# One fused attention and token-mixing kernel: the band of batch 0 added to its scores by matmuls, the local result turned mostly by whole-array matmuls, and another order of all steps

## The chip, the cores and the metric

The kernel runs on one core of one Trainium2 chip, as one program. The metric is device time in microseconds (us) of that core. Engines are named as in the profile: PE (TensorE matmul), PEld (its weight loads), DVE (VectorE), ACT (ScalarE), POOL (GpSimd), and SP, whose queue issues nearly all DMA transfers.

## The reference, cut to what matters

Inputs are q, k and v of 8 batches, 8 heads, 576 positions and head size 64, all float32, and four weights.

```python
def sm_attn(qq, kk, vv):                      # softmax(qq kk^T / 8) vv
    ...
q_d, k_d, v_d = means over groups of 4 positions
out_up    = np.repeat(sm_attn(q_d, k_d, v_d), 4, axis=2)
mask      = np.abs(pos[:, None] - pos[None, :]) < 4
scores    = np.where(mask, scale * np.matmul(q, k.transpose(0, 1, 3, 2)), -1e9)
out_local = np.matmul(softmax(scores), v)
x = (out_up + out_local).transpose(0, 2, 1, 3).reshape(B, S, H * D)   # 8 x 576 x 512

theta  = x @ w_theta                                                  # 512 x 512
zr, zi = x * np.cos(theta), x * np.sin(theta)
y = np.einsum('ts,bsd->btd', w_tok_r, zr) + np.einsum('ts,bsd->btd', w_tok_i, zi)
u = x + y
return u + np.maximum(u @ w_ch, 0.0)
```

So each position attends to at most seven neighbours (the band of half-width 3), and a coarse attention over 144 means is added to that. The result x goes through a phase mixing over the positions, and then over the channels.

## The kernel before, in words

Everything is computed in bfloat16 with float32 sums in PSUM. PSUM is one tile `PS` of 8 banks, and every step is told which banks it uses. The work of a batch is cut into small steps, each a function with a name of two letters:

- Loading: `lk`, `lq` (288 KB each, four per batch) and `lv`, `lw` (two halves of one chunk of v, 128 KB each) are issued on SP into 16 staging slots `st`. `ck`, `cq`, `cv` cast them to bfloat16 on DVE, ACT or POOL. For batch 0, v comes by `l1`, `c1`, `t1`, `e1`, `x1` instead.
- `tp` (line 302) transposes q and k by nine 128x128 matmuls; `ev` (line 315) copies the result from PSUM to `qT`, `kT`. Batch 7 does this by DMA (`dk`).
- Coarse attention: `qd`, `kd` (means), `pv`, `vd` (means of v), `sd` (scores, line 426), `ed` (exp, line 437), `nd` (times v, lines 447 and 452), `xn` (divide), `xd`, `xc` (turned, into `xdT`).
- Local attention: the 576 positions are cut into 10 blocks of 58 own positions, each seen through a window of 64; two blocks make a chunk, and the five chunks make three units of 2, 2 and 1 chunks. `ps` (line 482) makes the scores of a unit by matmuls of 64x64 on a quarter of the PE array. `ex` (line 490) takes the exponential of it all on ACT; `mk` (line 503 on POOL, line 505 on DVE) multiplies by `band`, a 0/1 tile. `po` (line 515) multiplies by v and, through a column of ones, makes the sums; `nm` (lines 523, 524) divides into `tmp`. `xt` (line 537) turns `tmp` so that channels lie on the partitions, again by 64x64 quarter-array matmuls; `xa` (line 545) adds the coarse result and writes `xT`.
- Mixing: `th` (line 556) and `tt` make theta, `cs` and `ct` its cosine and sine on ACT, `xm` turns x back, `zz` and `zt` (line 577) multiply, `mx` (line 636) mixes over positions with nine 128x128 by 288 matmuls, `ua` (line 641) adds x. `up`/`uc` or a DMA transpose `du` turn u, `ch` (line 666) multiplies by w_ch, `rl` (line 674) adds, `st` stores. `ht`, `rt`, `ss`, `sr` do the same for the last 64 positions of two batches together.
- The weights w_tok are loaded (`la`, `lb`, `lc`) and transposed (`wp`, `wc`) in the first part of the program. `wm` (line 764) are matmuls on a zero tile whose result nobody reads.

The order is written out by hand in the string `ORDER`: each word is a step's kind, then the PSUM banks, the engine or the staging slot. The n-th word of a kind is the n-th step of that kind (batch by batch). Each engine executes its instructions strictly in the order of the words, and waits where an operand isn't there yet or a buffer isn't free. Before the words, `constants` prepares `ident`, `band` and the rest. `te` and `ts` load ACT's tables.

## Time and profile before

| | |
|---|---|
| time, median of 3 runs | 230.32 us (229.73 to 231.82) |
| span of the profiled execution | 232.2 us |
| PE, PEld busy | 217.7 us (94%), 152.6 us (66%) |
| DVE busy | 187.7 us (81%) |
| ACT busy | 156.2 us (67%) |
| POOL busy | 145.0 us (62%) |
| HBM read, written | 33.98 MB, 9.44 MB |
| instructions | 9404 |

The profiled execution is known by its span, from the first to the last instruction of the trace; the page gives no other time for it. The span is 1.9 us (0.8%) longer than the median of the runs, and 0.4 us longer than the longest of them. Busy times count a matmul from its start to the modelled end of its pipeline, so neighbouring steps overlap: what a step costs PE is read from start to start. All places in the program are given in us from the start of the span.

### The profile page before, as it was taken

What the parts mean: (1) busy time and instruction counts of PE and PEld (TensorE: products, weight loads), DVE (VectorE), ACT (ScalarE), POOL (GpSimd) and SP (SyncE); (2) the same over time, 40 slices, a digit from 0 to 9 for tenths busy, and PEclk for the clock granted to TensorE, in tenths of its full rate; (3) what the DMA queues carried; (4) which work ended last, traced back from release to release, by engine and by line L of the source; (5) the groups of instructions that cost most, each with busy time, mean ns of one, the idle gap of its engine ahead of it and who ended that gap; (6) DMA issues with size and microseconds to landing.
All of it is one profiled execution on the core that took longest, in us unless ns stands there. A gap on an engine that the chain in (4) does not pass through costs nothing.

```text
span 232.2 us, 9404 instructions
## 1 busy us (share of the span) xinstructions
PE 217.7 (94%) x3943; PEld 152.6 (66%) x3970; DVE 187.7 (81%) x367; ACT 156.2 (67%) x243; POOL 145.0 (62%) x192
## 2 busy tenths in 40 slices
PE   7997899999999999899999989989998999999992
PEld 3655678877877666776775675756655775668741
DVE  5699888999988799789968887698986978558473
ACT  4589799689988898898877978778788232430000
POOL 7689977879985999879963489598952001100000
PEclk9999799999999999999999999999999999999999
DMA  6999968997999689968999996892284358656587
GB/s 217 395 390 390 291 114 238 361 300 118 265 391 179 165 245 285 243 142 214 205 165 347 307 213 115 206 153 92 67 149 109 71 127 193 138 159 137 142 227 245
DMA packets 76795, 49.41 MB, mean 213 GB/s; under 512 B 61136, under 2 KB 61392, under 8 KB 76752
## 3 DMA queue, kind: packets, MB, share of 16 engines
q1 hardware_dynamic: 76096, 47.76, 81.9%
q10 hardware_dynamic: 656, 1.05, 1.3%
q8 instruction: 31, 0.51, 0.9%
q14 instruction: 12, 0.10, 0.1%
HBM read 33.98 MB, written 9.44 MB: 187 GB/s over the span
## 4 chain that ended last, share of the span: by engine, by line
PE 60%; DMA 10%; POOL 10%; issue 6%; ACT 5%; DVE 4%; SPq 4%; DVEq 0%; POOLq 0%; ACTq 0%
PE PS L636 21%; PE PS L666 9%; PE PS L556 8%; DMA st<-in_q_dram 6%; PE PS L302 4%; POOL two L329 3%; PE PS L515 2%; SPq L347 2%; DMA st<-in_k_dram 2%; PE PS L537 2%; DMA ur<-uT 2%; POOL q_tm L295 2%; PE PS L482 2%; PE PS L447 1%; PE PS L595 1%
## 5 line engine op out<-in xcount | busy, mean ns | idle before, releaser
L636 PE MATMUL PS<-WT,z 128*128 128x288 bf16 x576 | 78.0, 287 | 0.0
L636 PEld LDWEIGHTS <-z 128*128 128x128 bf16 x576 | 53.9, 98 | 15.9 <-issue 1.3
L641 DVE TENSOR_TENSOR uT<-PS,xT 128x288 bf16<-128x288 f32 x64 | 28.6, 452 | 12.7 <-PE PS L636 10.9
L561 ACT ACTIVATE cs<-PS,pihc 128x512 bf16<-128x512 f32 x32 | 22.0, 689 | 21.1 <-PE PS L556 13.4
L556 PE MATMUL PS<-wth,xT 128*128 128x512 bf16 x116 | 30.8, 383 | 0.7 <-issue 0.2
L666 PE MATMUL PS<-wch,uT 128*128 128x512 bf16 (+1 forms) x122 | 29.8, 373 | 0.9 <-issue 0.6
L524 DVE TENSOR_TENSOR tmp<-PS,rl 128x512 bf16<-128x512 f32 x40 | 27.7, 692 | 1.4
L545 DVE TENSOR_TENSOR xT<-PS,xdT 128x928 bf16<-128x928 f32 (+1 forms) x24 | 22.3, 952 | 3.7 <-PE PS L537 2.3
L674 DVE SCALAR_TENSOR_TENSOR osb<-PS,ur 128x512 f32<-128x512 f32 x28 | 19.1, 687 | 7.1 <-DMA ur<-uT 3.0
L490 ACT ACTIVATE pm<-PS 128x1024 bf16<-128x1024 f32 (+1 forms) x24 | 20.5, 880 | 6.2 <-PE PS L482 6.1
L577 POOL TENSOR_TENSOR zT<-xT,cst 128x512 bf16<-128x512 bf16 x7 | 9.7, 1383 | 20.6 <-ACT cst L574 20.6
L295 POOL CAST k_tm<-st 128x576 bf16<-128x576 f32 x23 | 15.1, 668 | 11.2 <-DMA st<-in_k_dram 11.1
L396 POOL CAST v_w<-st 128x512 bf16<-128x512 f32 x21 | 13.3, 651 | 10.6 <-DMA st<-in_v_dram 10.5
L770 ACT ACT_TABLE_LOAD x15 | 19.2, 1283 | 0.3
L666 PEld LDWEIGHTS <-uT 128*128 128x128 bf16 x132 | 11.9, 98 | 11.2
L562 ACT ACTIVATE cs<-PS 128x512 bf16<-128x512 f32 x32 | 19.1, 597 | 0.0
L556 PEld LDWEIGHTS <-xT 128*128 128x128 bf16 x128 | 11.7, 99 | 10.6 <-issue 0.6
L295 POOL CAST q_tm<-st 128x576 bf16<-128x576 f32 x23 | 15.4, 686 | 4.9 <-DMA st<-in_q_dram 4.7
L503 POOL TENSOR_TENSOR pm<-pm,band 128x512 bf16<-128x512 bf16 x16 | 18.3, 1164 | 0.0
L329 POOL TENSOR_TENSOR two<-qT 128x576 f32<-128x576 bf16 x14 | 16.5, 1177 | 0.7 <-ACT qT L315 0.4
L620 DVE TENSOR_TENSOR z<-PS,cs 128x1024 bf16<-128x1024 bf16 x24 | 15.8, 684 | 0.5 <-ACT cs L562 0.3
L437 ACT ACTIVATE pd<-PS 128x864 bf16<-128x864 f32 x16 | 13.8, 889 | 2.5 <-PE PS L426 2.5
(124 smaller groups left out, 422.9 us busy)
## 6 DMA issues: line engine op xcount, KB each, us to landing
st<-in_k_dram SPq DMA_DIRECT2D x32, 288.0 KB, 6.5
st<-in_q_dram SPq DMA_DIRECT2D x32, 288.0 KB, 6.3
st<-in_v_dram SPq DMA_DIRECT2D x70, 128.0 KB, 5.2
out_dram<-osb SPq DMA_DIRECT2D x26, 256.0 KB, 4.0
st<-in_v_dram SPq DMA_DIRECT2D x4, 288.0 KB, 3.5
st<-in_moe_w_tok_r_dram SPq DMA_DIRECT2D x4, 288.0 KB, 6.5
st<-in_moe_w_tok_i_dram SPq DMA_DIRECT2D x4, 288.0 KB, 7.2
st<-in_moe_w_theta_dram SPq DMA_DIRECT2D x4, 256.0 KB, 6.7
```

The lines of the kernel that those rows point to most:

```text
L295: COPY[w](out=to, in_=of)
L329: nc.gpsimd.tensor_tensor(out=t, in0=src[:, :, 0:2], in1=src[:, :, 2:4], op=ALU.add)
L490: nc.scalar.activation(out=pm[(3 * b + u) % NPM][:, :, 0:n].rearrange("p e c j w -> p e (c j w)"), in_=at.pop(("ps", b, u))[:, :, 0:4 * W ...
L524: nc.vector.tensor_tensor(out=tmp[(NCH * b + c) % NTMP].rearrange("p g (j d) -> p g j d", d=D), in0=ps[:, :, :, 0:D], in1=r.unsqueeze(3).t ...
L545: nc.vector.tensor_tensor(out=xT[b % 2][:, :, lo:lo + cnt].rearrange("p e (m j) -> p e m j", j=4), in0=at.pop(("xt", b, u))[:, :, 0:cnt].r ...
L556: nc.tensor.matmul(out=ps, lhsT=xT[b % 2][:, dc, P * c:P * c + P], rhs=wth[:, dc, :], start=(dc == 0), stop=(dc == 3))
L561: nc.scalar.activation(out=t[:, 0, :], in_=ps, func=AF.Sin, bias=pihc, scale=1.0)
L562: nc.scalar.activation(out=t[:, 1, :], in_=ps, func=AF.Sin, bias=0.0, scale=1.0)
L636: nc.tensor.matmul(out=ps, lhsT=z[b % 2][:, j, P * dc:P * dc + P], rhs=WT[:, j, cols], start=(j == 0), stop=(j == 8))
L641: nc.vector.tensor_tensor(out=uT[b % 2][:, dc, cols], in0=at.pop(("mx", b, i)), in1=xT[b % 2][:, dc, cols], op=ALU.add)
L666: nc.tensor.matmul(out=ps[:, cols], lhsT=uT[b % 2][:, dc, P * c:P * c + P], rhs=wch[:, dc, cols], start=(dc == 0), stop=(dc == 3))
L770: nc.scalar.activation(out=idle, in_=pihc, func=TABLE[kind])
```

## The change

Three edits of the steps, and a new `ORDER`.

First, a tile `bneg` (0 inside the band, -1e9 outside) is made from `band` by the new step `kn`. For batch 0 `ps` first writes `bneg` into its PSUM banks by two matmuls per unit with the identity as weights, 512 columns each (256 in the last unit), and the 64x64 score matmuls then add to it. So `mk` has no steps for batch 0 any more.

Second, `xt` uses by default whole-array matmuls: per block two of them, each with 128 channels of `tmp` as weights and 2 x 58 columns of the identity. A `q` behind its banks keeps the 64x64 form, with other places in PSUM; `xa` reads both. Five of the 24 `xt` steps have the `q`.

Third, `tp` can be done with a `q` as 36 quarter-array transposes instead of nine whole ones. Two of its 28 steps have it.

The `wm` words go from 15,424 columns in all to 9,600. Steps of several kinds change their engine, among them `zt` (seven on POOL and one on DVE, now two on POOL and six on DVE). The words of `ORDER` are new from the first to the last; of them the diff below shows the first line only.

```diff
+HEAD = (0,)
+FAR = 1.0e9
 ORDER = """
-kcg l10 l11 l12 l13 kcv lk4 lq5 c1a wm7e0 kcg c1g t101 lk6 lk7 ckg c1a ckg c1v t123 e1a kcv e1v wm737 tp01 x12 cqa x13
+lk0 l11 l12 l13 ckv kcg l14 lk5 kcv kcg c1v ckg c1a c1a lq6 cqg wm001 wm001 wm001 wm0d0 t101 lq7 lk8 lk0 cqg ckg e1a
...
+    bneg = one([P, W], "bneg")
...
+    def kn(i, w):
+        EW[w].tensor_scalar(out=bneg, in0=band, scalar1=FAR, scalar2=-FAR, op0=ALU.mult, op1=ALU.add)
...
     def tp(b, i, n, w):
-        ps = at["tp", b, i, n] = pair(w).rearrange("p k e -> p (k e)").bitcast(BF16)
         t = tm[n][(2 * b + i) % TM]
-        for r in range(WR):
-            nc.tensor.transpose(out=ps[:, P * r:P * r + P], in_=t[:, r, :, :], identity=ident)
+        if w[2:] == "q":
+            ps = pair(w[:2]).bitcast(BF16)[:, :, 0:W * WR].rearrange("p a (r w) -> p r a w", w=W)
+            for r in range(WR):
+                for a in range(2):
+                    for x in range(2):
+                        nc.tensor.transpose(out=ps[W * x:W * x + W, r, a, :], in_=t[W * a:W * a + W, r, x, :],
+                                            identity=ident[W * a:W * a + W, W * a:W * a + W])
+        else:
+            ps = pair(w).rearrange("p k e -> p (k e)").bitcast(BF16)[:, 0:P * WR]
+            for r in range(WR):
+                nc.tensor.transpose(out=ps[:, P * r:P * r + P], in_=t[:, r, :, :], identity=ident)
+            ps = ps.rearrange("p (r a w) -> p r a w", a=2, w=W)
+        at["tp", b, i, n] = ps
...
     def psc(b, u, w):
         n = len(UNITS[u])
         ps = at["ps", b, u] = pair(w)
+        if b in HEAD:
+            for e in range(2):
+                nc.tensor.matmul(out=ps[:, e, 0:4 * W * n], lhsT=ident,
+                                 rhs=bneg.unsqueeze(1).to_broadcast([P, 4 * n, W]), start=True, stop=False)
...
-                            start=True, stop=True)
+                            start=(b not in HEAD), stop=(b not in HEAD or (i == n - 1 and hh == 3)))
...
     def xt(b, u, w):
-        ps = at["xt", b, u] = pair(w).rearrange("p k (x n) -> p (k x) n", x=2)
+        ps = pair(w[:2]).rearrange("p k (x n) -> p k x n", x=2)
+        quad = w[2:] == "q"
         for i, c in enumerate(UNITS[u]):
...
+                if quad:
+                    for j in range(4):
+                        for hf in range(2):
+                            r = slice(W * hf, W * hf + W)
+                            nc.tensor.matmul(out=ps[W * (j % 2):W * (j % 2) + W, hf, j // 2, cols],
+                                             lhsT=t[r, g, D * j:D * j + D], rhs=ident[r, W * hf + lo:W * hf + lo + OWN[n]],
+                                             start=True, stop=True)
+                    continue
+                for k in range(2):
+                    nc.tensor.matmul(out=ps[:, k, :, cols], lhsT=t[:, g, P * k:P * k + P],
+                                     rhs=identw[:, :, lo:lo + OWN[n]], start=True, stop=True)
...
-        mk=(mk, span(B, 3)), ...
+        mk=(mk, [x for x in span(B, 3) if x[0] not in HEAD]), ...
```

Two places of the new order, on the engines where the prediction needs them. The first is the queue of SP before the change, where it comes to the loads of batches 6 and 7 (`st<-in_q_dram` is a load of q, `64x8x64` the half of a chunk of v):

```order
L347 DMA st<-in_v_dram 64x8x64 x10
L287 DMA st<-in_k_dram 128x576 x2
L287 DMA st<-in_q_dram 128x576 x8
L347 DMA st<-in_v_dram 64x8x64
L287 DMA st<-in_k_dram 128x576
L680 DMA out_dram<-osb_120 128x512
```

The same stretch of SP's queue after the change:

```order
L364 DMA st<-in_v_dram 64x8x64 x5
L724 DMA_TRANSPOSE utr<-ut_115 128x4x128
L294 DMA st<-in_k_dram 128x576
L364 DMA st<-in_v_dram 64x8x64 x2
L294 DMA st<-in_q_dram 128x576
L294 DMA st<-in_k_dram 128x576 x2
L294 DMA st<-in_q_dram 128x576
L364 DMA st<-in_v_dram 64x8x64
L294 DMA st<-in_k_dram 128x576
L364 DMA st<-in_v_dram 64x8x64 x5
L294 DMA st<-in_q_dram 128x576 x2
```

Before, ten halves of v stand in one row ahead of two loads of k and eight of q; now the first q of batch 6 stands behind seven halves of v, and k, q and v alternate.

The second place is PE's own row, at the second unit's `xt` of batch 1, before the change (`tmp` holds the local result; the first rows of the step, and the one ahead of it):

```order
L636 MATMUL PS<-WT,z_103 128x288
L537 LDWEIGHTS tmp_88
L537 MATMUL PS<-ident,tmp_88 64x58
L537 LDWEIGHTS tmp_88
L537 MATMUL PS<-ident,tmp_88 64x58
```

And after the change:

```order
L665 MATMUL PS<-WT,z_103 128x288
L566 LDWEIGHTS tmp_88
L566 MATMUL PS<-ident,tmp_88 128x2x58
L566 LDWEIGHTS tmp_88
L566 MATMUL PS<-ident,tmp_88 128x2x58
```

In both the step follows a mixing step `mx`. It has 32 matmuls of 58 columns on quarters of the array before, and eight of 2 x 58 columns on the whole array after. In the whole program PE goes from whole-array steps to steps on a part of the array (`ps`, `po`, `sd`, `pv`, `x1`, and `xt` and `tp` in the quarter form) and back 51 times before, and 41 times after.

More of the change, by code (lines that the diff above doesn't have):

```diff
@@ new lines @@
+c1v kcv ckv lq9 lq2 wm230 t123 tp01 e1a eva x14 tp23 lb1 lq3 lb4 eva lk5 lk6 lb7 lb8 lq0 laa cqg x15 wm613 tp01 x12
+cvv kdv eva kng cvv cqg kdg cvv wm610 tp67 x10 x11 cvv eva cva qdv cba qdg ps45 pv67 vdv ps01 lb2 cbv ckg ckg lb9 lab
+la1 ex lac lkd cqg te cbg cbg cbg po45 lk5 sd23 lq6 lq3 lb8 lb2 ex nm lb7 ed lv4 ps67 sd01 po23 lve ed cqv lw ex tp45
+nd01 nm lw lv0 nd67 tp23 xn eva lw lvf eva xn wp4 po01 wca nm po67 xd5 xca wp2 xt01 cag kdg nm wca po34 xa wp5 xt67
+wp2 xa xm0 cag cbg caa nm wcv ts cag ckg th1 ckg cqg th7 xt34 tp56 cs cs xa zz wcv evv th1 cs tt7 xm2 xm0 ct cbg cbg
@@ L533, in xt @@
                 lo = STEP * n - W0[n]
-                for j in range(4):
-                    for hf in range(2):
-                        r = slice(W * hf, W * hf + W)
-                        nc.tensor.matmul(out=ps[W * (j % 2):W * (j % 2) + W, 2 * hf + j // 2,
-                                                CH * i + STEP * g:CH * i + STEP * g + OWN[n]],
-                                         lhsT=t[r, g, D * j:D * j + D], rhs=ident[r, W * hf + lo:W * hf + lo + OWN[n]],
-                                         start=True, stop=True)
+                cols = slice(CH * i + STEP * g, CH * i + STEP * g + OWN[n])
+                if quad:
[9 more added lines that the diff above has]
+                                     rhs=identw[:, :, lo:lo + OWN[n]], start=True, stop=True)
+        at["xt", b, u] = ps if quad else ps.rearrange("p k x n -> p x k n")
     def xa(b, u, w):
```

84 lines of the change are left out of this document (40 added, 44 removed).

## The prediction

> **What bounds the kernel now.** I read the busy time by stretches first (span of the stretch, then busy us and instructions of each engine, granted clock, DMA share, GB/s), with the page's line on the clock in 40 slices, to see which engine has no room left and where.
>
> ```profile
> PEclk9999799999999999999999999999999999999999
> core 0: us, PE busy (x) PEld busy (x) DVE busy (x) ACT busy (x) POOL busy (x), PEclk, DMA share, GB/s
> 20.00:37.00 17.00, 15.36 (x377) 12.53 (x379) 15.39 (x32) 14.86 (x24) 15.07 (x21) 0.90 0.86 234
> 37.00:120.00 83.00, 81.55 (x1735) 60.26 (x1743) 73.83 (x142) 70.54 (x105) 72.30 (x92) 1.00 0.98 238
> 120.00:141.00 21.00, 19.51 (x305) 14.04 (x306) 16.54 (x31) 17.61 (x30) 11.49 (x15) 1.00 1.13 261
> 141.00:206.00 65.00, 62.34 (x1104) 40.95 (x1115) 50.70 (x99) 38.12 (x65) 30.10 (x28) 1.00 0.61 131
> 206.00:232.20 26.20, 21.86 (x155) 14.97 (x153) 15.81 (x30) 1.61 (x4) 0.40 (x1) 1.00 0.68 187
> ```
>
> PE is the bound from 37 us on: idle 1.45 us of 83, then 1.49 of 21, then 2.66 of 65. Ahead of 37 us, where the first mixing step starts, DVE and ACT are as full as PE (15.39 and 14.86 of 17), and PE holds work that serves nothing. The stretch 120 to 141 is the leakiest: 7.1% idle, against 1.7% just before. The chain of waits and the instructions in order of time say why.
>
> ```profile
> 111.99 7.48 SPq L347 DMA_DIRECT2D st<-in_v_dram  x8
> 121.08 4.92 SPq L287 DMA_DIRECT2D st<-in_q_dram  x8
> 124.45 0.67 POOL L295 CAST k_tm<-st 128x576 bf16<-128x576 f32 x1 [4.29 <-DMA st<-in_k_dram]
> 134.20 0.66 POOL L295 CAST k_tm<-st 128x576 bf16<-128x576 f32 x1 [3.83 <-DMA st<-in_k_dram]
> 135.53 0.68 PE L302 MATMUL PS<-ident,q_tm 128*128 128x128 bf16 x9 [0.81 <-POOL q_tm L295]
> ```
>
> SP takes 7.48 us to issue eight halves of v; the loads of k and q for batches 6 and 7 queue behind them; POOL waits 4.29 and 3.83 us for k; and PE 0.81 us for a cast of q. That is a late load, not a lack of PE work.
>
> **What each edit costs on PE.** Durations of steps must be read from start to start:
>
> ```profile
> 75.97 0.45 PE L537 MATMUL PS<-ident,tmp 64*64 64x58 bf16 x32
> 76.35 1.28 PE L636 MATMUL PS<-WT,z 128*128 128x288 bf16 x9
> 77.56 0.44 PE L537 MATMUL PS<-ident,tmp 64*64 64x58 bf16 x32
> ...
> 165.83 0.42 PE L537 MATMUL PS<-ident,tmp 64*64 64x58 bf16 x32
> 166.08 0.33 PE L482 MATMUL PS<-qT,kT 64*64 64x64 bf16 x16
> ...
> 100.07 0.67 PE L302 MATMUL PS<-ident,k_tm 128*128 128x128 bf16 x9
> 100.57 1.27 PE L636 MATMUL PS<-WT,z 128*128 128x288 bf16 x9
> ...
> 110.11 1.28 PE L636 MATMUL PS<-WT,z 128*128 128x288 bf16 x9
> 111.22 0.61 PE L595 MATMUL PS<-ident,xT 128*128 128x128 bf16 x8
> ...
> 175.32 0.31 PE L537 MATMUL PS<-ident,tmp 64*64 64x58 bf16 x16
> 175.47 0.36 PE L426 MATMUL PS<-qd,kd 64*64 64x144 bf16 x12
> ```
>
> Going from the whole array to quarters costs 0.10: the same nine `mx` matmuls take 1.21 us (76.35 to 77.56) with quarters behind them and 1.11 (110.11 to 111.22) without. Going back costs 0.13: 32 quarter matmuls of `xt` take 0.38 us (75.97 to 76.35) when whole-array work follows, and 0.25 (165.83 to 166.08) when quarters follow. The 16 of the last unit take 0.15.
>
> On the whole array, nine 128-column matmuls take 0.50 us (100.07 to 100.57), 0.43 ns a column. A two-chunk `xt` of 8 x 116 columns is then 0.40 us, a one-chunk of 448 columns 0.19. So the streaming gets dearer: twelve two-chunk steps by +0.15 and seven one-chunk steps by +0.04, in all +2.1 us. In return PE changes its form 51 times each way before and 41 after: 10 x (0.10 + 0.13) = -2.3 us. Turning by the whole array is thus no gain by itself: -0.2 us, and what it has it owes to the order, which puts `xt` between whole-array steps. Two `tp` in quarters: 36 x 0.25/32 = 0.28 us for 0.50, together -0.4. PE's work falls by 0.6 us.
>
> **The band of batch 0.** `bneg` adds four matmuls of 512 columns and two of 256.
>
> ```profile
> 105.81 1.03 PE L556 MATMUL PS<-wth,xT 128*128 128x512 bf16 x4
> 106.67 0.39 PE L595 MATMUL PS<-ident,xT 128*128 128x128 bf16 x4
> ...
> 15.22 0.59 ACT L412 CAST vd<-PS 128x512 bf16<-128x512 f32 x1
> 15.69 0.74 ACT L415 CAST vd<-PS 32x256 bf16<-32x256 f32 x2
> 16.18 1.59 PE L764 MATMUL PS<-warm 128*128 128x512 bf16 x7 [0.16 <-issue]
> 16.45 1.94 ACT L490 ACTIVATE pm<-PS 128x1024 bf16<-128x1024 f32 x2
> 17.51 0.99 DVE L505 TENSOR_TENSOR pm<-pm,band 128x1024 bf16<-128x1024 bf16 x1
> 18.28 1.68 ACT L437 ACTIVATE pd<-PS 128x864 bf16<-128x864 f32 x2
> 18.56 0.32 PE L515 MATMUL PS<-v_w,pm 64*64 64x65 bf16 x16 [0.16 <-DVE pm L505]
> 19.50 2.26 POOL L503 TENSOR_TENSOR pm<-pm,band 128x512 bf16<-128x512 bf16 x2
> ...
> 22.91 0.42 PE L466 MATMUL PS<-ident,xdn 72*128 72x72 bf16 x8 [0.70 <-ACT kT L315]
> ```
>
> Four of 512 columns take 0.86 us (105.81 to 106.67), so +1.08 us in all. They need neither q nor k, stand ahead of the scores, and lie where PE now runs zero matmuls (16.18, 1.59 us) while ACT is busy: I take 0. Without that cover it is +1.08. Removed are 0.99 us of DVE and, with the third unit, about 3.4 of POOL (2.26 + half of it). But PE waited only 0.16 us for DVE's mask, and from 16.45 to 19.96 ACT's exponentials run back to back: the way to the end goes over ACT. So the mask's removal gives between 0 and -0.2 on the path; I take 0.
>
> **The start and the fill.** Ahead of the first scores ACT now makes all six copies from PSUM, where it made two and DVE four. ACT gives up three casts of q and k, three of v and the copies of `vd` for it.
>
> ```profile
> L315 ACT COPY kT<-PS 128x1152 bf16<-128x1152 bf16 x11 | 12.3, 1120 | 2.8 <-PE PS L302 2.4 <-POOL kd L332 0.3
> L295 ACT CAST q_tm<-st 128x576 bf16<-128x576 f32 x9 | 6.0, 679 | 0.4 <-DMA st<-in_q_dram 0.4
> L393 ACT CAST v_w<-PS 128x512 bf16<-128x512 f32 x4 | 2.1, 590 | 0.4 <-PE PS L388 0.4
> L577 DVE TENSOR_TENSOR zT<-xT,cst 128x512 bf16<-128x512 bf16 x1 | 0.8, 753 | 0.2 <-ACT cst L574 0.2
> L321 DVE TENSOR_REDUCE kd<-kT 128x290 bf16<-128x1160 bf16 x3 | 4.1, 1353 | 0.0
> L295 DVE CAST k_tm<-st 128x576 bf16<-128x576 f32 x2 | 1.5, 742 | 0.0
> ```
>
> That is 4 x 1.12 = +4.5 against 3 x 0.68, 3 x 0.59 and 0.59 + 0.74 us, together -5.1. Adding up all steps ahead of the first `mx` at such mean durations, DVE has +0.1 us and ACT +0.6 of some 30 each. These two pace the start, so the first `mx` comes where it did, within 1 us either way.
>
> The zero matmuls shrink by 5,824 columns, 2.4 us. They ran in waits, so 0 goes to the end. What they might hold up is the clock: in the fifth slice it is 0.7, and between 20 and 37 us the mean is 0.90, which is 17 x 0.10 = 1.7 us of lost clock, although the longest wait of PE there is the 0.70 at 22.91. The Trainium skill ("TensorE: Matmul & The Clock Gate", section "Why this matters for your kernels") asks only that PE have no idle gap over about 3 us; by it the shorter fill costs nothing and the sum below stays as it is. The row speaks otherwise: the clock fell without such a gap, so more such spells are a rival.
>
> **The order.** The loads of batches 6 and 7 no longer stand behind ten halves of v. Had 120 to 141 only the idle share of 37 to 120, PE would idle 0.37 us there instead of 1.49: -1.1. The bounds are 0, if the wait comes up elsewhere, and -1.5.
>
> **Sum.** -0.6 and -1.1 make -1.7 on the 232.2 us of the profiled span: 230.5. The median of the runs stands to that span as 230.32 to 232.2, 0.992. So I forecast 228.6 us. The tail is the same: the last mixing steps run in one row on PE, and behind the last matmul stand one pass of DVE and one store as before.
>
> **The rivals.**
>
> *The order closes more.* 20 to 37, 37 to 120 and 141 to 206 hold 1.64 + 1.45 + 2.66 = 5.75 us of idle PE. If half of that goes too, 230.5 - 2.9 = 227.6, or 225.8 in the runs. For it: all steps are placed anew, and ACT and POOL carry some 4 us less each by the step counts. Against it: most of these gaps are 0.3 to 1 us long and an order that closes one can open another.
>
> *The late load only moves.* Then only PE's -0.6 is left: 231.6, 229.7 in the runs. The new queue still has rows of five halves of v.
>
> *VectorE becomes the bound (slower).* DVE gets six `zt` at 0.75 us where it had one (+3.8), five more casts of q and k at 0.74 (+3.7), loses two means at 1.35 (-2.7) and two copies from PSUM of about as much (-2.7); masks are +0.9 (two more of other batches, one of batch 0 less) and the rest near nothing: about +3.0 us. It decides if DVE's 104 - 90.4 = 13.6 us of idle time between 37 and 141 are waits it can't use, since it executes in order. A full price, and no late load recovered: 231.6 + 3.0 = 234.6, or 232.7. Against it: 13.6 us is over four times the addition.
>
> *The clock (slower).* If the shorter fill lets the clock fall twice more in the start, at 1.7 us each: 230.5 + 3.4 = 233.9, or 232.0. For it: between the first scores and the first theta no zero matmuls are left at all. Against it: there DVE and ACT pace the start, and a slower PE may hide.
>
> **How the numbers follow.** A run of this kernel tells about 1% from no change: 228.0 to 232.6. The forecast's own range is 227.0 to 230.3, with a chance of 0.40 (0.18 of it under 228.0); more closed 0.21, all faster; only moved 0.13, all within; VectorE 0.15 (0.12 slower); the clock 0.11 (0.06 slower). That makes faster 0.39, within 1% 0.43, slower 0.18. The range goes from 224.8, inside the rival that closes more, to 233.5, past both slow ones and most of what the uncovered `bneg` would add; some 0.07 lies out at each side.
>
> **What would show it.** Right: a lone two-chunk `xt` takes 0.40 us from start to start and the `mx` ahead of it 1.11; POOL waits for k under 1 us each; PE idles under 0.7 us in any 21 us of the middle; the first `mx` starts at 36 to 38 us. Wrong: a first `mx` past 38; more than one slice of PEclk below 9; DVE above 90% from 37 to 141 with PE waiting for it at `zt` or the casts behind; new waits of PE for casts at other batches, above all behind the rows of v.

## The result and the profile after

The changed kernel takes 231.99 us (median of 20 runs, 230.74 to 235.13), the kernel before 230.35 us (median of 20 runs on the same chip, 229.00 to 231.87). The ratio is 1.0071, with a 95% interval from 1.0044 to 1.0098. Two later series with the same pair gave 1.0048 (1.0005 to 1.0090) and 1.0046 (1.0007 to 1.0084). So the change costs 0.5 to 0.7%, where a gain of 0.75% was forecast. Ratios here leave out runs that took over 1.5% more than the fastest of their kernel; medians hold all runs.

Single executions of one kernel differ more than that, and the profiled ones of this case did: the one after was the longest of its runs (235.13 us, with a spell of low granted clock in the start), and the one before, on which the prediction was built, had waits that another execution of the same kernel doesn't have. So I show another profile of both beside them, and call it the undisturbed one. Its execution took 229.22 us for the kernel before (span 227.5) and 230.40 for the changed one (span 228.7), each near 1 us below the median of its runs.

First the changed kernel in its first profile, with the clock in 40 slices and the busy time of the stretch with the spell (columns as in the prediction):

```profile
PEclk9999679999999999999999999999999999999999
20.00:37.00 17.00, 14.35 (x213) 11.12 (x213) 12.07 (x22) 11.44 (x21) 13.07 (x21) 0.80 0.96 253
```

The changed kernel in its undisturbed profile:

```profile
PEclk9999999999999999999999999999999999999999
20.00:37.00 17.00, 16.08 (x338) 12.51 (x327) 16.14 (x31) 15.71 (x26) 14.50 (x22) 1.00 1.00 256
37.00:120.00 83.00, 81.21 (x1612) 60.30 (x1609) 75.19 (x141) 67.87 (x107) 71.20 (x93) 1.00 0.96 239
120.00:141.00 21.00, 20.91 (x367) 15.30 (x366) 16.31 (x32) 16.84 (x26) 14.51 (x19) 1.00 0.83 217
```

And the kernel before in its undisturbed profile:

```profile
20.00:37.00 17.00, 15.18 (x383) 12.09 (x383) 16.22 (x32) 15.72 (x25) 15.61 (x21) 1.00 0.94 244
37.00:120.00 83.00, 82.87 (x1760) 61.21 (x1758) 73.79 (x144) 71.32 (x107) 73.95 (x93) 1.00 1.02 255
120.00:141.00 21.00, 21.00 (x355) 14.70 (x353) 18.46 (x36) 18.84 (x31) 15.93 (x18) 1.00 1.01 229
```

Two things are to be seen. The leak of 1.49 us between 120 and 141 us, which the prediction wanted to close, isn't there in the undisturbed profile of the kernel before: PE is busy 21.00 of 21. And between 37 and 120 us, where the kernel before leaves PE idle for 0.13 us, the changed one leaves 1.79.

Each execution can be cut in two at the first mixing step, which starts at 36.43 us before and at 36.12 after, in the undisturbed profiles. Behind it, up to the last matmul, the busy times are these, for the kernel before:

```profile
36.43:223.22 186.79, 186.06 (x3326) 130.44 (x3318) 154.84 (x297) 128.01 (x201) 116.07 (x135) 1.00 0.85 202
```

and for the changed one:

```profile
36.12:224.28 188.16, 186.21 (x3084) 132.46 (x3076) 157.34 (x300) 124.15 (x198) 114.43 (x138) 1.00 0.82 201
```

PE is busy for the same time (186.06 and 186.21 us), but idle 0.73 us before and 1.95 after. The start is no longer (0.3 us shorter), the tail behind the last matmul is 4.3 and 4.4 us. So the loss of 1.2 us between these two executions is waiting of PE. Of the changed kernel's 1.95 us, PE's row shows 1.72 in three places (the kernel before has 0.24 and 0.34 at two places of its own, 174.68 and 175.21):

```profile
67.80 0.45 PE L536 MATMUL PS<-v_w,pm 64*64 64x65 bf16 x32 [0.85 <-DVE tmp L545]
...
92.64 0.29 PE L464 MATMUL PS<-vd,pd 128*72 128x65 bf16 x4 [0.24 <-DVE osb L703]
...
98.03 1.28 PE L665 MATMUL PS<-WT,z 128*128 128x288 bf16 x9 [0.63 <-issue]
```

The first two come in all three profiles of the changed kernel, and in the version that has only the order and none of the other edits (0.86 and 0.21 there). The third comes in this profile alone; "issue" means that nothing in the trace is waited for, and the last section says what it is. VectorE's own row says what `po` waits for at 67.80:

```profile
64.55 0.46 DVE L670 TENSOR_TENSOR uT<-PS,xT 128x288 bf16<-128x288 f32 x1 [0.45 <-PE PS L665]
64.92 1.65 DVE L526 TENSOR_TENSOR pm<-pm,band 128x1024 bf16<-128x1024 bf16 x1
66.49 0.41 DVE L682 COPY ur<-PS 128x512 bf16<-128x512 bf16 x1
66.83 0.19 DVE L544 RECIPROCAL rl<-PS 128x8 f32<-128x8 f32 x1
67.05 0.69 DVE L545 TENSOR_TENSOR tmp<-PS,rl 128x512 bf16<-128x512 f32 x1
```

By the trace, `po` waits for the division into `tmp`, and that division stands behind a mask and a copy of `ur` in VectorE's row. VectorE isn't late as a whole (it waits 0.45 us just ahead): the division only stands too far back.

### The profile page after: what moved, and what is told of

Read it like the earlier page. It is cut to its first block, busy times and chain, and to the rows that moved or that the text cites. A ratio compares the mean times of both kernels' runs of the same rounds, so it can differ in the third digit from the quotient of the medians.

```text
span 233.4 us, 8765 instructions
## 1 busy us (share of the span) xinstructions
PE 221.6 (95%) x3648; PEld 155.9 (67%) x3648; DVE 187.6 (80%) x371; ACT 152.0 (65%) x235; POOL 141.4 (61%) x194
## 4 chain that ended last, share of the span: by engine, by line
PE 66%; DVE 14%; DMA 8%; issue 5%; ACT 3%; SPq 1%; POOL 0%; DVEq 0%; ACTq 0%; POOLq 0%
PE PS L665 27%; PE PS L585 10%; PE PS L695 9%; DMA st<-in_moe_w_tok_i_dram 3%; PE PS L536 3%; PE PS L317 3%; DMA st<-in_q_dram 3%; DMA st<-in_moe_w_tok_r_dram 3%; DVE osb L703 3%; DVE xT L573 2%; PE PS L566 2%; PE PS L503 2%; DVE z L649 2%; PE PS L464 1%; DVE uT L670 1%
## 5 line engine op out<-in xcount | busy, mean ns | idle before, releaser
L665 PE MATMUL PS<-WT,z 128*128 128x288 bf16 x576 | 79.3, 286 | 0.0
L585 PE MATMUL PS<-wth,xT 128*128 128x512 bf16 x128 | 33.3, 388 | 0.0
L695 PE MATMUL PS<-wch,uT 128*128 128x512 bf16 (+1 forms) x132 | 31.4, 373 | 0.0
L685 POOL COPY ut<-uT 128x256 bf16<-128x256 bf16 x5 | 2.4, 479 | 45.0 <-issue 27.6
L346 POOL TENSOR_TENSOR two<-qT 128x576 f32<-128x576 bf16 x14 | 17.0, 1212 | 13.6 <-ACT qT L332 7.8
L346 POOL TENSOR_TENSOR two<-kT 128x580 f32<-128x580 bf16 x15 | 17.6, 1176 | 5.1 <-ACT kT L332 4.5
L524 POOL TENSOR_TENSOR pm<-pm,band 128x512 bf16<-128x512 bf16 x14 | 16.3, 1185 | 4.1 <-ACT pm L511 4.1
L302 POOL CAST q_tm<-st 128x576 bf16<-128x576 f32 x25 | 16.9, 682 | 1.1 <-DMA st<-in_q_dram 1.0
L332 ACT COPY qT<-PS 128x1152 bf16<-128x1152 bf16 x11 | 12.4, 1124 | 4.3 <-PE PS L317 2.9
```

What stands on the lines that cost most here:

```text
L302: COPY[w](out=to, in_=of)
L346: nc.gpsimd.tensor_tensor(out=t, in0=src[:, :, 0:2], in1=src[:, :, 2:4], op=ALU.add)
L585: nc.tensor.matmul(out=ps, lhsT=xT[b % 2][:, dc, P * c:P * c + P], rhs=wth[:, dc, :], start=(dc == 0), stop=(dc == 3))
L665: nc.tensor.matmul(out=ps, lhsT=z[b % 2][:, j, P * dc:P * dc + P], rhs=WT[:, j, cols], start=(j == 0), stop=(j == 8))
L695: nc.tensor.matmul(out=ps[:, cols], lhsT=uT[b % 2][:, dc, P * c:P * c + P], rhs=wch[:, dc, cols], start=(dc == 0), stop=(dc == 3))
```

## The experiments

"The old order" is that of the kernel before.

**The kernel before once more**, unchanged.

> The kernel before once more, for a second profile of it. The changed kernel's two profiles differ by 3.7 us in span (233.4 and 229.7), and its runs take some 1.65 us more than their spans; by that the first profile of the kernel before (232.2) belongs to a run of about 233.9, over 3 us longer than its median. If so, a profile of a usual run has a span of 228 to 230 us, no spell of half clock, its first mixing step at 35.5 to 36.5 us, and the waits for k between 120 and 141 us (4.3 and 3.8 us on GpSimd, 0.8 on PE) are gone or below half. If the first profile is a usual one, span and waits are as they were, 232 us. Ratio 1.000.

230.08 us, ratio 0.9985 (0.9950 to 1.0019). The undisturbed profile above is its. POOL waits for k there too, in the order of time:

```profile
129.06 0.66 POOL L295 CAST k_tm<-st 128x576 bf16<-128x576 f32 x1 [3.91 <-DMA st<-in_k_dram]
```

and over the stretch from 20 to 206 us, in the groups of instructions (busy us, mean ns of one, idle time ahead):

```profile
L295 POOL CAST k_tm<-st 128x576 bf16<-128x576 f32 x19 | 12.8, 689 | 5.1 <-DMA st<-in_k_dram 5.1
```

The late load is real, 3.91 us at one cast where the expectation had it gone, and it costs PE nothing in this execution. Nor does it in another: of the eight profiles taken later of kernels in the old order, this one and seven of those below, none has PE waiting 0.2 us or more for a load or a cast of q or k between 120 and 141 us.

**The changed kernel once more**, unchanged, in two series.

> The changed kernel once more, with a fresh profile. In the profile of the first run the first mixing step stands at 40.6 us, 3.7 later than before, and PE's work behind it is 2.7 us shorter. Theory A (the order of the start makes the loss): the first mixing step stands at 39 us or later again, and PE is again without waits behind it; ratio to the kernel before 1.004 to 1.010. Theory B (the loss was the clock, which stood at half for 6.8 us in that one profile, against 3.4 before): a profile with one spell of half clock or none has its first mixing step at 37 to 38 us, and the ratio is then near 0.99 to 1.00.

> The changed kernel once more, as the one to compare with on the same chip: 231.4 to 232.2, ratio to the kernel before 1.004 to 1.009; first mixing step between 35.8 and 37.5 us, PE idle behind it 2 to 3 us where the kernel before had 0.7.

231.37 us, ratio 1.0048 (1.0005 to 1.0090), and 231.32 us, ratio 1.0046 (1.0007 to 1.0084). The first mixing step starts at 35.83 and 36.12 us; PE is idle behind it for 3.04 and 1.95 us. The load of k is in time now, in the same groups of its undisturbed profile:

```profile
L302 POOL CAST k_tm<-st 128x576 bf16<-128x576 f32 x20 | 13.3, 676 | 0.0
```

So the queue of SP does what its new row says, and in the undisturbed execution of the kernel before PE had not waited for that.

**The order alone.** The new words, but all `xt` in the quarter form, all `tp` on the whole array, and batch 0 masked.

```diff
-HEAD = (0,)
+HEAD = ()
 # in ORDER: every xt with q, no tp with q, no kng
-la1 ex lac lkd
+la1 ex mkv lac lkd
-lb8 lb2 ex nm lb7
+lb8 lb2 ex mkg nm lb7
-ed cqv lw ex tp45
+ed cqv lw ex mkg tp45
```

> The new order with the old forms of all steps: xt all in quarters, tp all on the whole array, band of batch 0 by masks (on the engines and beside the steps where they stood). If the loss of the change lies in the order of the steps, it is slower than before by about what the all-quarters version was, ratio 1.015 to 1.022. If the order is as good as the old one and the new forms make the loss, ratio 0.998 to 1.005.

235.08 us, ratio 1.0217 (1.0169 to 1.0265). The new order by itself loses 2.2%, and the new forms of the steps give back 1.5 to 1.7% of it. Its first mixing step starts at 39.27 us, 3.2 later than in the changed kernel's undisturbed profile. The next three runs say which form does what.

**`xt` in the quarter form, in the new order.**

> The changed kernel with all 24 xt in the quarter form, in the new order. By the prediction's prices (streaming 0.25 for 0.40 us, but 0.10 + 0.13 for going to quarters and back; nearly all of the 19 stand between whole-array steps) it is 19 x 0.23 = 4.4 us of changes of form against 2.1 of streaming: 2.3 us slower than the changed kernel, ratio to before about 1.017. If the whole-array form is no gain even there, the time is the same within 0.5 us, ratio about 1.007.

```diff
-xt01 ... xt67 ...
+xt01q ... xt67q ...    # all 24
```

234.55 us, ratio 1.0181 (1.0122 to 1.0240), 3.2 us above the changed kernel in the same series. Of these, 2.3 us lie ahead of the first mixing step (38.13 us against 35.83), and PE shows why:

```profile
25.61 0.42 PE L483 MATMUL PS<-ident,xdn 72*128 72x72 bf16 x8 [1.00 <-issue]
...
31.53 0.22 PE L561 MATMUL PS<-ident,tmp 64*64 64x54 bf16 x3 [1.17 <-issue]
```

Only the second of them stands in an `xt`. The first comes ahead of the first `xt` of the program, where the changed kernel has the same instructions and stands still for 1.70 us in its first profile, 0.32 in its second and not at all in its third. So up to 1.0 of the 3.2 us may be this execution's and not the form's. Behind the first mixing step PE's busy time is 187.40 us, 0.9 more than in the changed kernel of the same series (186.52) and 1.2 more than in the undisturbed one, and PE waits once more, 1.26 us at 80.77, for VectorE's `xT`.

**All `xt` on the whole array, in the old order.** The functions `xt` and `xa` of the changed kernel in the kernel before.

> The kernel before with all 24 xt as whole-array matmuls, old order. By the prediction's prices: 16 two-chunk steps at +0.15 and 8 one-chunk at +0.04 of streaming, +2.7 us; and most xt of the old order stand beside other quarter steps, so few changes of form go away (some are added): time longer by 2 to 4 us, ratio 1.009 to 1.017. If the whole-array form is cheaper than priced (the quarter form pays for its many instructions), ratio 1.000 or less.

231.68 us, ratio 1.0059 (1.0031 to 1.0086).

```profile
36.73:225.91 189.18, 188.51 (x2906) 133.54 (x2898) 156.59 (x297) 128.29 (x201) 115.70 (x135) 1.00 0.81 199
```

PE's busy time behind the first mixing step rises by 2.45 us (188.51 against 186.06) and its idle time stays at 0.67: the streaming is dearer, as priced, and the old order, where `xt` stand beside other quarter steps, saves one change of form each way for it (50 instead of 51). By the runs it costs 1.4 us, less than the 2 to 4 that were expected.

**The mask for batch 0 again, in the new order.** Only the edits of `HEAD` and of the three `mk` words above, and no `kn`.

> The changed kernel with the band of batch 0 applied by the mask again (one multiplication on VectorE, two on POOL) and without the bneg matmuls; order and turning of the local result as changed. Theory A (the bneg matmuls lie in time in which PE would wait, and the new order has room for them): 231.5 to 233.5, ratio 1.005 to 1.013, since POOL and VectorE get the masks back in their full start. Theory B (the bneg matmuls cost their 1.08 us on the way to the end): 230.3, ratio 1.000, first scores 0.5 us earlier. The forecast had 0 for both sides: 231.4.

233.89 us, ratio 1.0174 (1.0128 to 1.0220).

```profile
20.55 0.43 PE L536 MATMUL PS<-v_w,pm 64*64 64x65 bf16 x16 [3.53 <-DVE pm L526]
```

In the new order PE waits 3.53 us for the mask, since VectorE's row is full ahead of it; the first `po` starts at 20.55 us instead of 18.23. On top of it the clock falls:

```profile
PEclk9997999999999999999999999999999999999999
```

Right behind the wait it stands at half for 3.4 us, and the mean granted clock is 0.983 to 0.993 in all six runs. In the version with the order alone PE waits 3.37 us at the same place, the clock is at half for 6.8 us, and the six runs have 0.981 to 0.992, against a mean of 0.994 to 0.997 in the changed kernel's three series. So the 2.2% of the order alone are in part this wait and the clock behind it. The new order depends on `bneg`.

**`bneg` in the old order**, first beside all zero matmuls, then in their place.

```diff
 # first version, in ORDER of the kernel before: no mk for batch 0, and
-kcv e1v wm737
+kcv e1v kng wm737
 # second version: made on VectorE, 2560 columns of zero matmuls less
-kcv e1v kng wm737
+kcv knv e1v wm737
-wm624 ps01
+ps01
-wm656 wm717
+wm632 wm717
```

> The kernel before with the band of batch 0 added by matmuls instead of the mask; old order, with its zero matmuls. By the prediction the 1.08 us of matmuls lie in a wait, and the mask was not on the way: ratio 0.998 to 1.002. If the matmuls lie on the way (the changed kernel's first scores come 0.7 us later than before), ratio 1.003 to 1.005; if the mask held up the start, 0.995.

> The kernel before with the band of batch 0 by bneg matmuls, as in the earlier run, but the 2560 columns of bneg now take the place of 2560 columns of zero matmuls (1280 ahead of the first scores, 1280 behind the second), and bneg is made on VectorE, where it is idle. Theory A (the earlier run lost 2.9 us because the zero matmuls that were to be the cover of bneg were left in, and POOL made bneg ahead of its casts): 230.3 to 231.3, ratio 1.000 to 1.004. Theory B (bneg lies on the way by itself): 231.5 and over, ratio 1.005 to 1.012.

First 233.52 us, ratio 1.0125 (1.0065 to 1.0184); then 231.00 us, ratio 1.0045 (1.0003 to 1.0087). The prediction hid `bneg` behind the zero matmuls. In the first version they are left in, and more is lost. But its six runs fall apart, three from 231.55 to 232.66 us and three from 234.38 to 234.59, and the profile is of one of the latter. In it PE waits 0.79 us for a cast of k whose load comes late, ahead of every edit, and stands still for 1.84 us at 31.83 with nothing in the trace that it waits for. So a part of the 1.25% isn't the matmuls of `bneg`. The second version changes the fill and the engine of `bneg` at once, so which of the two saves how much is not shown. In it `bneg` is nearly hidden, and still no gain over the mask.

**The fill back into the new order.** 5,120 columns of zero matmuls more, at three places.

```diff
-ps45 pv67 vdv ps01 lb2
+ps45 pv67 vdv ps01 wm224 lb2
-ed lv4 ps67 sd01
+ed lv4 ps67 wm030 sd01
-nd67 tp23 xn
+nd67 tp23 wm544 xn
```

> The changed kernel with 5,120 columns of zero matmuls put back between the first scores of batch 0 and the first transposes of w_tok, about as many as stood there before. Theory B (the clock): no more than one spell of half clock, theta's matmuls at 0.216 us each, time shorter by 1 to 2 us, ratio about 1.000. Theory A (the order): the clock may be better, but the steps are in the same waits and up to 1 us of fill lies on the way; ratio 1.005 to 1.012.

233.10 us, ratio 1.0112 (1.0072 to 1.0152), 1.7 us slower than the changed kernel in the same series. The first mixing step started at 38.11 us, 2.3 later than in the changed kernel of the series. The mean granted clock over the runs was 0.997, against 0.995 without this fill. If that is more than chance, the fill buys some clock; it doesn't buy time.

**The first transposes of w_tok later.** Four `wp` and their copies go behind theta.

```diff
-xn wp4 po01 wca nm po67 xd5 xca wp2 xt01 cag kdg nm wca po34 xa wp5 xt67 wp2 xa xm0
+xn po01 nm po67 xd5 xca xt01 cag kdg nm po34 xa xt67 xa xm0
...
-cs tt7 xm2 xm0 ct cbg cbg
+cs tt7 wp4 wca wp5 wca xm2 xm0 ct cbg wp6 wcv wp4 wcv cbg
```

> The changed kernel with four of the nine transposes of w_tok (the first four wp and their wc) moved behind the theta steps of batch 0, where they stood before the change; all else as in the changed kernel. Theory A1 (PE, which runs in order, waits in the first of them for a late load of w_tok, and the steps of batch 0 queue behind it): the first xt comes 1 to 2 us earlier than at 27.15, and the time falls by 1 to 2 us, ratio to before about 1.000. Theory A2 (they only fill time in which PE would wait anyway for the division of batch 0): first xt within 0.5 us, and the four transposes come on top later, time the same or up to 1.5 us longer, ratio 1.007 to 1.014.

233.38 us, ratio 1.0105 (1.0034 to 1.0177), with the first mixing step at 37.25 us. Their early place filled time in which PE would have waited anyway.

**PE's waits behind the first mixing step.** Three versions of the new order. The first moves four waits away:

```diff
-mx6 mx7 qdg mkv ua po45 ps01 ex ex cva kdg qdg cvg cvg ua nm mx6 cvg
+mx6 mx7 qdg ua mkv mx6 po45 ps01 ex ex cva kdg qdg cvg cvg ua nm cvg
-po45 po67 ccg lv8 lw cka lq0 lw lve lw lv1 nm lw up0 mx3 nd12
+mx3 po45 po67 ccg lv8 lw cka lq0 lw lve lw lv1 nm lw up0 nd12
-mkv ed vda zz tp01 zp4 ckg nd23 rl
+mkv ed vda rl zz tp01 zp4 ckg nd23
-cs tt2 evv xn ct
+cs tt2 xn evv ct
```

> The changed kernel with four small moves in its order, no work added or taken away: (1) at 38.9 us the third mixing step of batch 0 goes ahead of the po of batch 1 that waits 0.65 us for VectorE's mask, and the first ua ahead of that mask; (2) at 69.1 us a mixing step goes ahead of the po that waits 0.85 us for tmp; (3) at 94.0 us the output step rl goes ahead of zz on VectorE, since nd waits 0.24 us for it; (4) at 159.8 us the division xn goes ahead of the 2 us copy of qT on VectorE, since ps waits 0.36 us for it. Theory A (what the new order loses behind the first mixing step is PE waiting for VectorE at these places): PE from first mixing step to last matmul takes 187.1 us instead of 189.2, the time falls by 1.5 to 2.1 us, to 229.5 to 230.3, ratio to the kernel before 0.996 to 1.000. Theory B (VectorE as a whole is the bound there and a wait that is taken away comes up a little later): 231.2 to 231.9, ratio 1.004 to 1.007, new PE waits of together 2 us elsewhere.

233.25 us, ratio 1.0129 (1.0068 to 1.0190): no gain, theory A falls, and it is slower than theory B had it, too. All four waits are gone, and others stand in their place:

```profile
33.91 0.68 PE L317 MATMUL PS<-ident,q_tm 128*128 128x128 bf16 x9 [0.50 <-POOL q_tm L302]
...
41.88 0.38 PE L443 MATMUL PS<-qd,kd 64*64 64x144 bf16 x12 [0.74 <-POOL v_w L413]
```

and in sum behind the first mixing step:

```profile
37.29:226.65 189.36, 187.05 (x3084) 132.51 (x3076) 157.51 (x300) 123.97 (x196) 113.90 (x138) 1.00 0.81 199
```

PE is idle 2.31 us behind the first mixing step, between the 1.95 and 3.04 of the changed kernel. (The wait at 33.91 lies ahead of every move; that start is 1.2 us longer with the same instructions, so part of its loss is this execution's.)

The second puts the six `zt` of VectorE back on POOL, the third takes three copies of transposes and a cast of q from VectorE to ACT:

```diff
-ztv          # second version, six times
+ztg
-evv ... evv ... cqv ... evv     # third version, between 50 and 70 us
+eva ... eva ... cqa ... eva
```

> The changed kernel with all zt on POOL (six went from POOL to VectorE in all; 0.75 us each on VectorE, 1.15 on POOL). Theory A (PE loses at four places where VectorE's row stands in an unlucky order, VectorE has room elsewhere): within 0.5 us of the changed kernel, 231.0 to 232.0, ratio 1.003 to 1.007. Theory B (VectorE is too full between 36 and 141 us): 4.5 us of VectorE work gone, time falls by 1.5 to 2.5 us to 229 to 230.5, ratio 0.994 to 1.000.

> The changed kernel with three copies of transposes (1.35 us each) and one cast of q (0.74) between about 50 and 70 us moved from VectorE to ACT (3 x 1.12 + 0.68 us there). Theory A (VectorE's row is too full between 36 and 95 us): 4.8 us of VectorE gone, PE's waits for VectorE at 69 and 94 us vanish and nothing takes their place, 1.0 to 2.0 us faster than the changed kernel in the same call. Theory B (it is the place of single steps, every engine's row is in order and about equally loaded): within 0.7 us of the changed kernel either way, with new PE waits for ACT of about the size of those that went.

238.53 us, ratio 1.0359 (1.0305 to 1.0412), and 234.37 us, ratio 1.0180 (1.0137 to 1.0224). Both take work from VectorE and both are slower. With `zt` on POOL, first POOL's row, then PE's:

```profile
85.84 1.16 POOL L606 TENSOR_TENSOR zT<-xT,cst 128x512 bf16<-128x512 bf16 x1 [4.12 <-ACT cst L603]
...
94.76 0.29 PE L424 MATMUL PS<-v_w,pu 128*32 128x256 bf16 x2 [2.10 <-POOL v_w L413]
```

POOL stands still for 4.12 us, since `zt` waits for ACT's cosines, and all that is queued behind it comes late, a cast of v among it, for which PE waits 2.10. With the copies on ACT, the cosines themselves come late, and then VectorE's `zt` behind them:

```profile
54.81 0.38 PE L624 MATMUL PS<-ident,xT 128*128 128x128 bf16 x4 [1.26 <-ACT cs L591]
...
61.52 0.40 PE L616 MATMUL PS<-ident,zT 128*128 128x128 bf16 x4 [0.65 <-DVE zT L606]
```

So less work on VectorE alone doesn't make PE wait less: the work went to POOL or ACT, and the steps behind it there came late. Each row is executed in order, and each step that is moved delays what stands behind it. That VectorE's load plays no part at all is not shown, since no version took work from it without giving it to another engine.

**Quarter transposes in the old order.** By the prices of the prediction, a `tp` that stands beside a quarter-array step saves 0.22 us in the quarter form, and 0.45 between two. Seven of them in the old order, where PE hardly waits, should give 1.8 us.

```diff
 # ORDER of the kernel before; tp and ev as in the changed kernel
-tp67 eva eva xd0 ... tp45 xt67 ... tp67 cka ts ... tp56 ps12 ... tp67 lv7 ... tp23 eva xm0 ... tp01 sd67
+tp67q eva eva xd0 ... tp45q xt67 ... tp67q cka ts ... tp56q ps12 ... tp67q lv7 ... tp23q eva xm0 ... tp01q sd67
```

> The kernel before, in its old order, with seven of its tp steps in the quarter form, all behind the first mixing step and each beside a quarter-array step: one between two quarter steps (tp45 between po and xt), three with one ahead, three with one behind. Prices from the traces: a whole tp 0.50 us, a quarter one 0.28 from start to start; a change of form out of quarters 0.13, into quarters 0.10. With one quarter neighbour the number of changes stays as it was, so 0.22 is saved, with two 0.22 + 0.23 = 0.45: together -1.8 us. Theory A (PE is the bound in the old order, so what PE saves comes out at the end): 228.4 to 229.0, ratio 0.991 to 0.995, PE from first mixing step to last matmul 185.0 to 185.5 instead of 186.8. Theory B (the work of PE is not what sets the time, casts and transfers are): no change, ratio 0.998 to 1.002, PE waits up by 1.5 us.

> The version with seven quarter transposes once more. If its stalls belong to its row of instructions: ratio 1.009 to 1.018 as before, stalls at 50, 70 and 125 us again, together 3 to 4 us. If they were chance: ratio under 1.005 and no stall at these three places.

233.59 us, ratio 1.0136 (1.0091 to 1.0181), and once more 233.75 us, ratio 1.0128 (1.0082 to 1.0174). The steps do take less (10.47 us of PE for all `tp` behind the first mixing step before, 9.27 now), but PE stands still, in the first execution

```profile
49.58 0.31 PE L547 MATMUL PS<-ident,tmp 64*64 64x58 bf16 x15
52.43 0.46 PE L547 MATMUL PS<-ident,tmp 64*64 64x58 bf16 x33 [2.54 <-issue]
...
69.83 0.38 PE L525 MATMUL PS<-v_w,pm 64*64 64x65 bf16 x21 [0.73 <-issue]
...
125.42 0.32 PE L525 MATMUL PS<-v_w,pm 64*64 64x65 bf16 x16 [0.95 <-issue]
```

and in the second at the same places:

```profile
52.41 0.46 PE L547 MATMUL PS<-ident,tmp 64*64 64x58 bf16 x33 [2.32 <-issue]
...
69.81 0.38 PE L525 MATMUL PS<-v_w,pm 64*64 64x65 bf16 x21 [0.80 <-issue]
...
127.22 0.32 PE L525 MATMUL PS<-v_w,pm 64*64 64x65 bf16 x16 [1.72 <-issue]
```

The stall at 52 us comes in the middle of one `xt`, after 15 or so of its matmuls, twice at the same one. It belongs to the row of instructions, then, and not to a load that is late by chance.

The same with only the four that stand alone (the three between 47 and 54 us whole again):

> The kernel before, in its old order, with only four of the seven tp steps in the quarter form: those that stand alone beside one quarter-array step (between pv and xm, zp and ps, ch and pv, mx and sd); the three between 47 and 54 us, which stood in one dense run with the quarter xt, are whole again. Theory A (PE runs out of instructions in dense runs of small ones): the stall of 2.54 us at 50 us is gone, PE saves 4 x 0.22 = 0.9 us, and the time is 229.4 to 230.5, ratio 0.995 to 1.000, if the stalls at 70 and 125 us go too, and 230.5 to 231.5, ratio 1.000 to 1.005, if those two stay. Theory B (a quarter tp costs more than its price wherever it stands): 232 and over, ratio 1.007 and over, stalls of over 2 us in all.

> The version with four quarter transposes once more. Theory A (dense runs are what stalls PE; four alone do no harm): 229.4 to 230.6, ratio 0.995 to 1.001, and as in its first profile no PE stall over 0.5 us without a cause behind the first mixing step. Theory B (also four in the quarter form make PE run out of instructions in most executions): 232 and over, with such stalls of over 1.5 us.

The first series gave 230.06 and 229.63 us and then four times between 233.70 and 238.14, too far apart for a ratio; its profile had no such stall. The second series gave 233.05 us, ratio 1.0093 (1.0052 to 1.0134), with stalls elsewhere:

```profile
31.36 0.64 PE L578 MATMUL PS<-xT,wth 128*128 128x64 bf16 x16 [1.14 <-issue]
...
67.60 0.22 PE L525 MATMUL PS<-v_w,pm 64*64 64x65 bf16 x2 [0.87 <-issue]
```

The stall at 52 us is gone with the dense run, as theory A had it, but the version is slower all the same: theory A is right on the place and wrong on the time. The stall at 31.36 us stands ahead of the first edited step, so it isn't these steps' doing. In both profiles the tail is 1.3 us longer too (5.6 us), with VectorE waiting for a DMA transpose (`utr<-ut`), which no edit touches. So why the four cost so much in most runs stays open. None of the versions beats the kernel before.

## Why the prediction was wrong, point by point

- **The late load, -1.1 us: the step that failed.** "Had 120 to 141 only the idle share of 37 to 120, PE would idle 0.37 us there instead of 1.49" took the gap of one execution for the kernel's. In the undisturbed profile PE idles 0.00 us there although POOL still waits 3.91 us for k. There was nothing to recover, in this or in any of the seven other profiles in the old order. Even in the first profile the gap was not all late load: of its 1.49 us the wait for the cast of q, which the prediction shows, is 0.81, and another third is a stall of the last section's kind:

```profile
120.36 0.33 PE L650 MATMUL PS<-ident,uT 128*128 128x128 bf16 x3 [0.50 <-issue]
```

  The rival that the late load only moves had the right term, 0.
- **The base, 0.992.** The profiled execution was 2% longer than the undisturbed one (232.2 and 227.5 us of span). A run's time is 1.7 us above its span (229.22 and 227.5, 230.40 and 228.7), so the span was set beside the wrong number: that execution took near 233.9 us, 3.6 above the median. I scaled the sum by the ratio of median to span, which keeps a gap that another execution lacks, only smaller.
- **PE's work, -0.6 us: the second term that failed.** Most of its prices held step by step. In the undisturbed profile of the changed kernel a lone two-chunk `xt` and its neighbours read

```profile
144.86 0.39 PE L679 MATMUL PS<-ident,uT 128*128 128x128 bf16 x4
145.08 1.27 PE L665 MATMUL PS<-WT,z 128*128 128x288 bf16 x9
146.18 0.58 PE L566 MATMUL PS<-ident,tmp 128*128 128x116 bf16 x8
146.60 1.26 PE L665 MATMUL PS<-WT,z 128*128 128x288 bf16 x9
```

  0.42 us for `xt` (0.40 forecast), 1.10 for the `mx` ahead (1.11 forecast); a one-chunk `xt` takes 0.20 (0.19). All `tp` behind the first mixing step take 10.27 us from start to start in the order alone and 9.98 in the changed kernel, so the two quarter ones save 0.29 in themselves (0.4 forecast with the change of form that the step ahead is spared). The twelve and the seven `xt` are 0.02 and 0.01 dearer than priced. Yet the total is +0.15 us of busy PE between the undisturbed profiles, not -0.6, and the version with the order alone shows where it went. With the old forms in the new order PE is busy for 187.92 us behind the first mixing step, 1.86 more than before; three more changes of form each way there (45 for 42) are 0.7 of it, and the rest stays open. From there to the changed kernel, with 31 changes, the prices give -3.2 for the form, +1.7 for the streaming and -0.4 for `tp`, together -1.9, and measured is -1.7 (186.21). So the prices were right, and what failed is that the new order was taken to cost PE no work. That the form owes what it has to its place is seen from both sides, by the medians: +1.4 us in the old order, -3.2 in the new, though in the profiles the -3.2 are waits and stalls more than work.
- **`bneg`, taken as 0.** Its matmuls take 0.53 us for each of two units (15.54 to 16.07) and 0.32 for the third, 1.38 us where 1.08 was priced. The 0.30 between them is what three changes into quarters cost at 0.10 each, since the 64x64 scores follow directly:

```profile
15.54 0.60 PE L496 MATMUL PS<-bneg,ident 128*128 128x512 bf16 x2
16.07 0.56 PE L503 MATMUL PS<-qT,kT 64*64 64x64 bf16 x32
```

  In the new order it pays, since without it PE waits 3.53 us for the mask; in the old order it costs 0.45% with the fill taken out and 1.25% in the version with the fill left in. So 0 was right at most for the changed kernel.
- **The first mixing step where it was, within 1 us.** Right: 36.43 us before, 35.83 and 36.12 after. The 40.64 us of the first profile is mainly the spell of low clock (6.8 us at half) and one stall of 1.70 us.
- **The fill and the clock.** The fill was worth nothing, as forecast: more of it was slower by 1.7 us. The rival of the clock gave 232.0 us, next to the measured 231.99, but that is luck: between the undisturbed profiles, both at a clock of 1.00, the 1.2 us are there without it. A part of the rest may be the clock, whose mean over the runs is about 0.002 lower for the changed kernel in both later series (0.995 and 0.997 against 0.997 and 0.999). The spells of low clock come in single executions of either order. The Trainium skill ("TensorE: Matmul & The Clock Gate", section "Why this matters for your kernels") ties a slower clock to gaps of over some 3 us. The two waits of 3.37 and 3.53 us for the mask agree with it; but the first profiles of both kernels had spells with no wait of PE over 1.70 us in the start, so the rule doesn't explain these, and what does is open.
- **VectorE, the rival on the slow side.** Half right. It named waits of PE for VectorE and a slower kernel; VectorE's busy time behind the first mixing step rose by 2.5 us (154.84 to 157.34; +3.0 forecast). But its mechanism, a VectorE too full, isn't borne out: 4.8 us less on it made the kernel slower, if at ACT's cost. At 67.80 and 92.64 the place of single steps in rows that run in order decided.
- **What I left out: the step that turned the sign.** The sum had no term for new waits of PE in an order in which every step is placed anew; I named them under what would be wrong and gave them no price. They are +1.1 us in all three profiles of the changed kernel (0.85 and 0.24); in all, PE idles 1.1 to 2.3 us more behind the first mixing step than the 0.73 of the kernel before. With the late load at 0, the work at +0.15, these waits and a start 0.3 us shorter, the sum is near the +1.2 us between the undisturbed profiles and the 0.6 to 1.6 us between the medians of the three series.

Three attempts to take the new waits away made others; which of them an order could avoid altogether stays open.

## What to carry to other kernels

Read a second execution before a gap in the profile becomes a term of the sum: a wait of another engine, however long, is worth only what the bound engine loses by it in most runs. Where one engine is busy 99% of a stretch, an edit is worth what it does in that order: the same form of `xt` cost 1.4 us in one order and saved up to 3.2 in the other. And count instructions beside busy time: a step that is cheaper and has four times the instructions can stall the engine that runs it.

## What the hardware showed that I had not expected

PE stands still at fixed places of its own row of instructions. Counting the weight loads and matmuls in the trace ahead of each "issue" stall of 0.3 us or more, from 15 us on, in the twelve executions (of nine kernels) that have one, gives this (place in us, stall in us, instructions ahead, and their distance from 951 in units of 256):

```
kernel                         place   stall  ahead  (ahead-951)/256
before                          24.12  0.65    696    -1.00
before                         120.36  0.50   4779    14.95
after                           26.18  1.70    699    -0.98
after, 2nd profile              24.75  0.32    699    -0.98
after, 2nd profile              45.32  0.55   1467     2.02
after, 3rd profile              98.03  0.63   3514    10.01
xt in quarters, new order       25.61  1.00    699    -0.98
xt in quarters, new order       31.53  1.17    955     0.02
whole xt, old order             24.79  0.59    698    -0.99
bneg beside the fill            31.83  1.84    954     0.01
bneg beside the fill            80.46  0.57   3002     8.01
mask in the new order           54.91  0.35   1723     3.02
mask in the new order          121.64  1.26   4281    13.01
four steps to ACT               18.75  0.37    444    -1.98
four steps to ACT              121.60  1.01   4281    13.01
seven quarter tp                52.43  2.54   1978     4.01
seven quarter tp                69.83  0.73   2746     7.01
seven quarter tp               125.42  0.95   5303    17.00
seven quarter tp, again         52.41  2.32   1974     4.00
seven quarter tp, again         69.81  0.80   2741     6.99
seven quarter tp, again         76.01  0.57   2997     7.99
seven quarter tp, again        127.22  1.72   5290    16.95
four quarter tp, again          24.61  0.54    696    -1.00
four quarter tp, again          31.36  1.14    951     0.00
four quarter tp, again          67.60  0.87   2485     5.99
four quarter tp, again         101.86  0.48   4014    11.96
```

Every stall, 26 of 26, stands within 13 instructions of a step of 256. (The traces of the last two lack some 28 matmul records each, so their late counts are a little low.) The page's part on DMA queues has the other half, for the kernel before in its undisturbed profile:

```profile
q8 instruction: 31, 0.51, 1.0%
```

and for the changed one:

```profile
q8 instruction: 28, 0.46, 0.9%
```

Each of these pieces is 16 KB, and there is one for every 256 to 261 of PE's instructions (7,940 in 31 pieces, 7,296 in 28; 6,980 in 27 with the whole `xt` in the old order). So PE's program comes in by DMA, 256 instructions at a time, while it runs, and PE waits where the next piece isn't there yet. The times of the pieces bear it out. Take the first piece of this queue for the step at 439 instructions, the second for 695, and so on: in all 26 stalls PE goes on 1.3 to 1.8 us after the piece of its step has landed, and at none of the 573 steps of the twenty traces was PE five instructions past the step less than 1.2 us after the landing. The Trainium skill ("Runtime: NRT & Kernel Launch", section "What's in a NEFF") calls PE's stream one of raw 64-byte instructions; 16 KB is 256 of those, and the distances in the table agree. In the traces a piece takes 0.9 to 2.5 us to come in. In the stalls it starts 1.0 to 5.3 us after PE has passed the step before: there, a piece comes no more than one step ahead. At the stall ahead of 52.43, PE had used its 256 instructions in 3.45 us, while the piece started after 3.35, took 1.02, and PE went on 1.62 later. In the quarter form PE uses 64 instructions in 0.25 us. A change anywhere in PE's row thus moves all later boundaries, into a dense run of small steps or out of it. That explains why the version with seven quarter transposes lost more than it saved: in its two profiles these stalls take 4.2 and 5.4 us. What delays the start of a piece in one execution and not in the next, no run here shows.
